# Turning the second tile's tokens through DRAM instead of on TensorE

## The chip, the cores and the metric

The kernel runs on one core of a Trainium2 chip. The metric is the device time of one execution in microseconds. TensorE does the matmuls, VectorE, ScalarE and GpSimd the element work, and SP (SyncE) issues nearly all the DMAs, one after another in the order of its own queue.

## The reference

Chunked attention over 8 batches of 576 tokens and 8 heads, followed by a gated feed-forward block over the 4608 tokens that come out of it:

```python
scores = scale * np.matmul(q_c, k_c.transpose(0, 1, 2, 4, 3))   # chunks of 64 tokens
attn = np.exp(scores - np.max(scores, axis=-1, keepdims=True))
attn = attn / (np.sum(attn, axis=-1, keepdims=True) + 1e-09)
out = np.matmul(attn, v_c)
x = out.transpose(0, 2, 1, 3).reshape(4608, 512)
xn = x / np.sqrt(np.mean(x * x, axis=-1, keepdims=True) + 1e-06) * rms_g
g = xn @ w_gate                                                  # 512 x 1536
silu = g * (1.0 / (1.0 + np.exp(-g)))
return (silu * (xn @ w_val)) @ w_out                             # 1536 x 512
```

## The kernel before

The tokens are worked off in nine tiles of 512. A tile consists of two units of 256 tokens, and a unit of two blocks of 128. Tiles 0, 1 and 2 are plain: for each of the 12 blocks `f` of the hidden width, `gate_and_value` makes two sums of 12 matmuls each (`ps_g`, `ps_v`), `gated` turns them into the product `sg` and splits it into a high and a low half (`gh`, `gl`), and `down` adds 12 matmuls to the four output sums `acc`. `down` of block f - 1 follows the gate of block f. At the end of a tile `evacuate` copies the four sums out, by turns on VectorE and ScalarE, and SP stores them (`out_dram<-o`). The six later tiles go in pairs with fewer products per pair; they read weights that were saved to DRAM (`wsd`, `osd`) during tiles 0 to 2.

Every product of full precision is made of three matmuls on high and low halves. Tile 0 therefore also converts the weights: the `conv_...` steps load 18 raw tiles (`raw`, 1 MB each) and split them into `parts`, with four operations a tile on VectorE (lines 201, 209, 217, 243) and three on ScalarE. Copies of the weights go to DRAM as `wfd`, `wsd` and `osd`.

The tokens of a tile are made by attention while the tile before is multiplied. Units 2 and 3 make tile 1, during tile 0; units 4 and 5 make tile 2, during tile 1; unit 6 belongs to the first pair and is begun at the start of tile 2: its loads are written at step 0 of that tile, its scores after the gate of f = 0. A unit loads `qt`, `kt` and `vt` (`load_unit`, 512 KB each, into the pool `io` of four buffers), makes scores, a softmax and the values, and `norm_unit` or `turned_norm` scales the rows. The matmuls want the tokens turned, with the model width on the partitions. For units 2 and 3 `norm_unit` writes into the tile `x`, GpSimd multiplies by the root mean square (line 517), and `x_transpose` turns 128 x 128 blocks on TensorE into PSUM at the end of tile 0, half of them ahead of the `down` of f = 10 and half ahead of that of f = 11. `x_split` then makes the halves `xh` and `xl`. For units 4 and later `turn_x` transposes 32 x 32 blocks in place on VectorE (line 458), sends the tile to DRAM (`away_x`), and `turn_x_back` fetches it in four reads of 32 partitions each, which land turned in `x`; there `x_split` works from `x`.

In tile 0 a scheduler sets the order on all engines. From tile 1 on TensorE keeps the order in which the code is written; the scheduler still orders SP, and may put a load ahead of work that is written earlier.

## Time and profile before

| What | Value |
|---|---|
| Median of three runs | 899.58 us (897.92 to 899.82) |
| Profiled execution, its own time | 898.29 us |
| Its span, first to last instruction | 896.5 us |
| TensorE busy | 880.0 us, 98% of the span |
| VectorE, ScalarE, GpSimd busy | 607.6, 454.1 and 185.7 us |
| Share of TensorE in the chain that ended last | 94% |
| Mean granted clock of TensorE | 0.991 |

Of 40 equal slices TensorE is full in 38; the first is the start-up. VectorE is full only in slices of tile 0, up to about 112 us. Tile 1 runs from 138 to 242 us, tile 2 begins there.

### The profile page before, as it was taken

What the parts mean: (1) busy time and instruction counts of PE and PEld (TensorE: products, weight loads), DVE (VectorE), ACT (ScalarE), POOL (GpSimd) and SP (SyncE); (2) the same over time, 40 slices, a digit from 0 to 9 for tenths busy, and PEclk for the clock granted to TensorE, in tenths of its full rate; (3) what the DMA queues carried; (4) which work ended last, traced back from release to release, by engine and by line L of the source; (5) the groups of instructions that cost most, each with busy time, mean ns of one, the idle gap of its engine ahead of it and who ended that gap; (6) DMA issues with size and microseconds to landing.
All of it is one profiled execution on the core that took longest, in us unless ns stands there. A gap on an engine that the chain in (4) does not pass through costs nothing.

```text
span 896.5 us, 17443 instructions
## 1 busy us (share of the span) xinstructions
PE 880.0 (98%) x6828; PEld 720.6 (80%) x6828; DVE 607.6 (68%) x965; ACT 454.1 (51%) x772; POOL 185.7 (21%) x157
## 2 busy tenths in 40 slices
PE   5999999999999999999999999999999999999998
PEld 4778888888888888888887888888878888888886
DVE  6999955364568745985677997556769953334776
ACT  5988934253446464454456645435547522222452
POOL 0004050342200000233233003333330014323200
PEclk8899999999999999999999999999999999999999
DMA  9889999777978855698977877677667794445442
GB/s 349 328 318 336 332 337 347 239 255 235 303 252 234 267 170 196 250 298 294 320 240 265 318 301 286 245 277 249 232 231 286 281 355 171 152 154 199 179 165 95
DMA packets 85794, 231.84 MB, mean 259 GB/s; under 512 B 8912, under 2 KB 45264, under 8 KB 71504
## 3 DMA queue, kind: packets, MB, share of 16 engines
q1 hardware_dynamic: 84656, 230.20, 73.1%
q8 instruction: 54, 0.88, 0.4%
q10 hardware_dynamic: 1056, 0.52, 0.2%
q14 instruction: 28, 0.23, 0.1%
HBM read 167.25 MB, written 63.44 MB: 257 GB/s over the span
## 4 chain that ended last, share of the span: by engine, by line
PE 94%; DVE 2%; ACT 2%; DMA 0%; issue 0%; POOL 0%; ACTq 0%; DVEq 0%
PE ps_b L857 11%; PE ps_a L857 11%; PE ps_c L857 11%; PE acc L664 11%; PE ps_g L627 11%; PE ps_v L627 10%; PE ps_b L1070 6%; PE ps_c L1070 6%; PE ps_d L857 5%; PE ps_a L1070 5%; PE ps_d L1070 3%; PE ps_o L426 2%; PE ps_s L299 2%; PE ps_o L484 1%; DMA x<-qT_dram 0%; ACT raw L196 0%
## 5 line engine op out<-in xcount | busy, mean ns | idle before, releaser
L857 PE MATMUL ps_b<-xp,wr 128*128 128x512 f32 x432 | 104.7, 391 | 0.1
L857 PE MATMUL ps_c<-xp,wr 128*128 128x512 f32 x432 | 104.0, 390 | 0.0
L857 PE MATMUL ps_a<-xp,wr 128*128 128x512 f32 x432 | 103.8, 390 | 0.0
L627 PE MATMUL ps_g<-xh,parts 128*128 128x512 f32 x288 | 97.2, 399 | 0.1
L857 PEld LDWEIGHTS ps_b<-xp,wr 128*128 128x128 f32 x432 | 80.5, 188 | 17.4 <-issue 0.5
L857 PEld LDWEIGHTS ps_c<-xp,wr 128*128 128x128 f32 x432 | 80.9, 188 | 16.9
L627 PE MATMUL ps_v<-xh,parts 128*128 128x512 f32 x288 | 94.5, 389 | 0.0
L857 PEld LDWEIGHTS ps_a<-xp,wr 128*128 128x128 f32 x432 | 80.8, 188 | 17.0
L664 PE MATMUL acc<-parts,gh 128*128 128x512 f32 x288 | 90.2, 394 | 0.0
L945 POOL TENSOR_TENSOR g<-u,u 128x512 f32<-128x512 f32 x18 | 23.2, 1289 | 251.9 <-DVE u L941 141.3
L627 PEld LDWEIGHTS ps_g<-xh,parts 128*128 128x128 f32 x288 | 54.7, 190 | 12.7 <-ACT parts L237 0.6
L627 PEld LDWEIGHTS ps_v<-xh,parts 128*128 128x128 f32 x288 | 54.1, 188 | 11.2
L977 ACT CAST gh<-g 128x512 fp32r<-128x512 f32 x72 | 43.6, 622 | 37.8 <-PE ps_c L1070 13.5
L664 PEld LDWEIGHTS acc<-parts,gh 128*128 128x128 f32 x288 | 53.1, 188 | 11.3
L982 DVE TENSOR_TENSOR gl<-g,gh 128x512 fp32r<-128x512 f32 x72 | 49.3, 692 | 16.2 <-PE ps_a L1070 5.7
L913 ACT ACTIVATE p<-p 128x512 f32<-128x512 f32 x36 | 22.7, 632 | 70.0 <-POOL p L935 60.4
L935 POOL TENSOR_TENSOR p<-p,p 128x512 f32<-128x512 f32 x36 | 46.9, 1313 | 53.9 <-DVE rs L387 35.6
L627 PE MATMUL ps_g<-xl,parts 128*128 128x512 f32 x144 | 56.8, 395 | 0.1
L664 PE MATMUL acc<-parts,gl 128*128 128x512 f32 x144 | 56.1, 390 | 0.0
L627 PE MATMUL ps_v<-xl,parts 128*128 128x512 f32 x144 | 56.0, 389 | 0.0
L922 DVE TENSOR_TENSOR u<-ps_b,p 128x512 f32<-128x512 f32 x36 | 24.6, 687 | 41.5 <-PE ps_b L857 38.0
L857 PE MATMUL ps_d<-xp,wr 128*128 128x512 f32 x216 | 52.3, 391 | 0.0
(151 smaller groups left out, 1706.7 us busy)
## 6 DMA issues: line engine op xcount, KB each, us to landing
wr<-wsd SPq DMA_DIRECT2D x63, 1024.0 KB, 7.0
wo<-osd SPq DMA_DIRECT2D x30, 1024.0 KB, 7.6
raw<-w_up_dram SPq DMA_DIRECT2D x12, 1024.0 KB, 9.5
vt<-v_dram SPq DMA_DIRECT2D x18, 512.0 KB, 7.2
wsd<-parts SPq DMA_DIRECT2D x18, 512.0 KB, 8.3
qt<-qT_dram SPq DMA_DIRECT2D x17, 512.0 KB, 5.6
kt<-kT_dram SPq DMA_DIRECT2D x17, 512.0 KB, 6.6
away_e<-e SPq DMA_DIRECT2D x28, 256.0 KB, 3.5
```

Of the source, the lines that this page charges most:

```text
L299: nc.tensor.matmul(st["s"][j][c * CH : (c + 1) * CH, pr], st["q"][rows, pr, tok : tok + CH], st["k"][rows, pr, tok : tok + CH], start=True ...
L426: nc.tensor.matmul(st["o"][(2 * c + t) * Q : (2 * c + t + 1) * Q, h * D : (h + 1) * D], eT[c][rows, t, h], vt[rows, c, h], start=True, sto ...
L627: nc.tensor.matmul(ps, a[f][:, cols], b[dt], start=(dt == 0 and i == 0), stop=(dt == NDT - 1 and i == 2),)
L664: nc.tensor.matmul(acc[s], a[:, cols], b, start=(f == 0 and i == 0), stop=(f == NF - 1 and i == 2),)
L857: nc.tensor.matmul(ps, w[:, a, m, cols], xp[:, b, kt], start=start and kt == 0 and i == 0, stop=stop and kt == 1 and i == 2, skip_group_ch ...
L913: nc.scalar.activation(t, t if src is None else src, AF.Silu)
L922: nc.vector.tensor_tensor(kp["u2"], b["b"], kp["p1"], op=add)
L935: nc.gpsimd.tensor_tensor(kp["p5"], kp["p1"], kp["p5"], op=add)
L945: nc.gpsimd.tensor_tensor(g[:, 0, 1], kp["u2"], kept[0]["u2"], op=mult)
L977: nc.scalar.copy(gh, src)
L982: nc.vector.tensor_tensor(gl, src, pair[0].bitcast(F32), op=ALU.subtract)
L1070: nc.tensor.matmul(banks[m][name], w[:, (0, 1, 0)[k], m * P : (m + 1) * P], (gh, gh, gl)[k], start=opens and i == 0 and k == 0, stop=not ( ...
```

## The change

Units 2 and 3 go the way of units 4 and later. `norm_unit` writes into a new tile `xu` of the pool `io`, which then holds four buffers for each unit; `turn_x` and `turn_x_back` of unit 2 are called at f = 7 and f = 8 of tile 0, those of unit 3 both at f = 10. `x_transpose` is gone. At f = 11 of tile 0 the gate's tail and the four splits are put in written order on ScalarE and VectorE. Unit 3's multiplication by the root mean square moves from GpSimd to ScalarE, unit 2's stays. The host undoes the changed order of tokens in the output from tile 1 on instead of tile 2.

```diff
-        first = 2 * u % NSUB
-        xu = x[:, first : first + 2]
-        xv = xu.rearrange("p s (j b a d) -> p j s b a d", j=2, b=2, d=Q)
+        xu = state["xu", u] = io.tile([P, 4, NDT, 2, Q], F32, tag="io", name="xu")
+        xv = xu.rearrange("p q (j b) s d -> p j s b q d", b=2)
+        xs = xu.rearrange("p q a s d -> p s (q a) d")
...
         for s in range(2):
-            nc.gpsimd.tensor_scalar(xu[:, s], xu[:, s], ri[:, s : s + 1], None, op0=ALU.mult)
+            if shared:
+                nc.scalar.mul(xs[:, s], xs[:, s], ri[:, s : s + 1])
+            else:
+                nc.gpsimd.tensor_scalar(xs[:, s], xs[:, s], ri[:, s : s + 1], None, op0=ALU.mult)
...
-    def x_transpose(dts):
-        for dt in dts:
-            pt = bank(ps_a, "ps_x")
-            for s in range(NSUB):
-                nc.tensor.transpose(
-                    pt[:, s * P : (s + 1) * P], x[:, s, dt * P : (dt + 1) * P], ident
-                )
-            x_split(dt, pt, slice(0, TT))
...
+    def next_tokens():
+        for dt in range(NDT):
+            x_split(dt, blocks(x)[:, :, dt], slice(0, TT))
...
+            elif t == 0 and f == NF - 1:
+                ps_last = gate_and_value(f)
+                with tc.manual_schedule(engines={mybir.EngineType.Activation, mybir.EngineType.DVE}):
+                    g = gated(f, CONVS[f % 2], conv_step, ps_last)
+                    next_tokens()
...
-                    norm_unit(u, o)
-                if f == NF - 1:
-                    x_transpose((0, 1))
+                    norm_unit(u, o, u == 3)
+                if f in (7, 10):
+                    turn_x(2 + (f == 10))
+                if f in (8, 10):
+                    turn_x_back(2 + (f == 10), x)
...
-        if t == 0:
-            x_transpose((2, 3))
```

**VectorE after the values of unit 3, in tile 0.** `ps_o` are unit 3's values, lines 209, 217 and 243 convert weights, the first `sg` and `gl` belong to f = 9. Before:

```order
L505 TENSOR_TENSOR x<-ps_o_1220,rs_u 128x2x128 x2
L209 SCALAR_TENSOR_TENSOR w<-w,raw 128x1024
L243 TENSOR_TENSOR parts<-w,parts 128x1024
L217 SCALAR_TENSOR_TENSOR w<-raw,w 128x1024
L209 SCALAR_TENSOR_TENSOR w<-w,raw 128x1024
L243 TENSOR_TENSOR parts<-w,parts 128x1024
L217 SCALAR_TENSOR_TENSOR w<-raw,w 128x1024
L651 TENSOR_TENSOR sg<-ps_v,sg 128x512
L243 TENSOR_TENSOR parts<-w,parts 128x1024
L656 TENSOR_TENSOR gl<-sg,gh 128x512
```

After:

```order
L505 TENSOR_TENSOR xu<-ps_o_1224,rs_u 128x2x4x32 x2
L209 SCALAR_TENSOR_TENSOR w<-w,raw 128x1024
L243 TENSOR_TENSOR parts<-w,parts 128x1024
L217 SCALAR_TENSOR_TENSOR w<-raw,w 128x1024
L201 TENSOR_SCALAR w<-w 128x1024
L458 STREAM_TRANSPOSE xu<-xu 128x1024
L209 SCALAR_TENSOR_TENSOR w<-w,raw 128x1024
L645 TENSOR_TENSOR sg<-ps_v,sg 128x512
L217 SCALAR_TENSOR_TENSOR w<-raw,w 128x1024
L650 TENSOR_TENSOR gl<-sg,gh 128x512
L243 TENSOR_TENSOR parts<-w,parts 128x1024 x2
```

One conversion tile's work has moved behind the `sg` of f = 9, and a clamp (line 201) and the block transpose of `xu` stand ahead of it.

**SP in tile 0, around a pair of raw weight loads.** `wsd` are stores of converted weights, `wfd` copies of the weights, `qt` and `kt` the loads of unit 3. Before:

```order
L222 DMA wfd_133<-w 128x1024
L182 DMA raw<-w_up_dram 128x1024 x2
L687 DMA wsd_141<-parts 128x4x256
L687 DMA wsd_143<-parts 128x4x256
L222 DMA wfd_134<-w 128x1024
```

After:

```order
L222 DMA wfd_133<-w 128x1024
L182 DMA raw<-w_up_dram 128x1024 x2
L267 DMA qt<-qT_dram 128x1024
L268 DMA kt<-kT_dram 128x1024
L222 DMA wfd_134<-w 128x1024
```

The loads of unit 3 stand where two stores were; before they stood far ahead of these rows, and the two stores are now earlier.

**SP at the end of tile 1.** `away_x` and the reads back are unit 5's tokens, the first `qt` is the load of unit 6, the one behind `out_dram` that of unit 7. Before, a stretch around the loads and one around the stores:

```order
L754 DMA w<-wfd_139 128x1024
L267 DMA qt<-qT_dram 128x1024
L461 DMA away_x_2423<-xu 128x1024
L268 DMA kt<-kT_dram 128x1024
L269 DMA vt<-v_dram 128x1024
L468 DMA x<-away_x_2423 32x4x256 x4
L778 DMA wsd_160<-side 128x512
```

```order
L780 DMA wsd_159<-w 128x2x256
L967 DMA out_dram<-o 128x512 x4
L267 DMA qt<-qT_dram 128x1024
L849 DMA wr<-wsd_140 128x2048
L268 DMA kt<-kT_dram 128x1024
```

After, the same two stretches:

```order
L748 DMA w<-wfd_139 128x1024
L461 DMA away_x_2422<-xu 128x1024
L681 DMA wsd_157<-parts 128x4x256
L681 DMA wsd_159<-parts 128x4x256
L681 DMA wsd_160<-parts 128x4x256
L736 DMA osd_162<-parts 128x2x256
L736 DMA osd_165<-parts 128x2x256
L736 DMA osd_171<-parts 128x2x256
L468 DMA x<-away_x_2422 32x4x256 x4
L772 DMA wsd_160<-side 128x512
```

```order
L774 DMA wsd_159<-w 128x2x256
L961 DMA out_dram<-o 128x512 x4
L267 DMA qt<-qT_dram 128x1024
L268 DMA kt<-kT_dram 128x1024
L269 DMA vt<-v_dram 128x1024
L267 DMA qt<-qT_dram 128x1024
L843 DMA wr<-wsd_140 128x2048
```

The three loads of unit 6 have moved from ahead of the reads to behind the four output stores, where the first `qt` is now unit 6's and the second unit 7's; six stores of weights stand between unit 5's way out and its reads.

## Rows read from the trace of the kernel before

**Rows 1.** The page's busy times: engine, us, share of the span, instructions.

```profile
PE 880.0 (98%) x6828; PEld 720.6 (80%) x6828; DVE 607.6 (68%) x965; ACT 454.1 (51%) x772; POOL 185.7 (21%) x157
```

**Rows 2.** Waits of TensorE: us in total, times, longest; first and last of five.

```profile
PE ps_s L299 <- DMA x<-qT_dram: 5.6, 2, 5.1
...
PE ps_a L1070 <- DVE gl L982: 0.3, 1, 0.3
```

**Rows 3.** Timeline of TensorE, end of tile 0: start us, us, line, operation.

```profile
131.02 1.03 PE L533 MATMUL ps_x<-ident,x 128*128 128x128 f32 x8
...
138.24 0.39 PE L627 MATMUL ps_g<-xh,parts 128*128 128x512 f32 x1
```

**Rows 4.** The chain that ended last, in order of time: one undisturbed `down` block.

```profile
123.02 2.72 PE acc L664 x12
```

**Rows 5.** Instructions on tile `xu` up to 220 us: ns min/median/max.

```profile
L452 ACT ACTIVATE xu<-xu,ri x2: 712/718/724, 183.1 to 184.2; 128x512 f32<-128x512 f32 x2
L458 DVE STREAM_TRANSPOSE xu<-xu x1: 1246/1246/1246, 184.9 to 184.9; 128x1024 f32<-128x1024 f32 x1
```

**Rows 6.** Timeline, 114 to 121 us.

```profile
114.55 5.63 POOL L517 TENSOR_SCALAR x<-x,ri_u 128x512 f32<-128x512 f32 x2
...
118.75 0.68 DVE L651 TENSOR_TENSOR sg<-ps_v,sg 128x512 f32<-128x512 f32 x1
...
120.14 0.39 PE L627 MATMUL ps_v<-xh,parts 128*128 128x512 f32 x1
```

**Rows 7.** DMA issues by line, whole run: count, KB each, median us to landing.

```profile
away_x<-xu SPq DMA_DIRECT2D x14, 512.0 KB, 3.0
x<-away_x SPq DMA_DIRECT2D x56, 128.0 KB, 4.3
```

**Rows 8.** Timeline, 66 to 80 us.

```profile
67.55 1.18 SPq L687 DMA_DIRECT2D wsd<-parts  x2
...
78.59 1.16 PE L299 MATMUL ps_s<-kt,qt 64*64 64x64 f32 x64
```

**Rows 9.** DMA issues near 33.6, 68, 233 and 245 us: us to landing.

```profile
qt<-qT_dram SPq DMA_DIRECT2D x1, 512.0 KB, 10.0
...
wsd<-parts SPq DMA_DIRECT2D x2, 512.0 KB, 11.5
...
x<-away_x SPq DMA_DIRECT2D x1, 128.0 KB, 5.6
...
qt<-qT_dram SPq DMA_DIRECT2D x1, 512.0 KB, 3.7
```

**Rows 10.** Timeline of SP's issues, 224 to 246 us.

```profile
224.78 0.45 SPq L267 DMA_DIRECT2D qt<-qT_dram  x1
...
231.70 1.75 SPq L468 DMA_DIRECT2D x<-away_x  x4
...
245.33 0.44 SPq L267 DMA_DIRECT2D qt<-qT_dram  x1
```

**Rows 11.** Timeline, 239 to 249 us.

```profile
239.75 2.56 ACT L524 ACTIVATE xh<-x,g_col 128x512 fp32r<-128x512 f32 x4
...
242.31 0.39 PE L627 MATMUL ps_g<-xl,parts 128*128 128x512 f32 x1
...
247.62 1.16 PE L299 MATMUL ps_s<-kt,qt 64*64 64x64 f32 x64
```

**Rows 12.** Busy times, 220 to 240 us; last: clock, DMA share, GB/s.

```profile
220.00:240.00 20.00, 20.00 (x113) 16.52 (x98) 8.89 (x14) 8.70 (x19) 6.63 (x6) 1.00 1.02 315
```

**Rows 13.** Tile `kt`: us from issue to landing over all its loads.

```profile
DMA to landing us min/median/max: 3.5/6.6/9.4
```

**Rows 14.** Three start-up stretches; the clock is third from the end.

```profile
16.00:18.00 2.00, 0.66 (x4) 0.42 (x4) 1.86 (x6) 1.36 (x3) 0.12 (x1) 0.87 0.99 418
28.00:30.00 2.00, 1.91 (x5) 1.42 (x5) 2.00 (x6) 2.00 (x5) 0.00 (x0) 0.50 0.96 389
30.00:32.00 2.00, 2.00 (x8) 1.53 (x7) 1.93 (x3) 1.96 (x3) 0.00 (x0) 0.72 0.81 330
```

## Prediction

> **What bounds the kernel now.** I read the busy times first. TensorE is busy for 880.0 us, 98% of the span [rows 1]. Next comes the list of what TensorE waited for: its five entries add up to 12.3 us and all but the last lie in the start-up, before the long matmuls of tile 0 begin [rows 2]. After that it waits 0.3 us in all. So the time is the sum of what stands in TensorE's own queue, and only two things can move it: instructions taken out of that queue, or a new wait put into it. A saving on VectorE, ScalarE or GpSimd is worth nothing here, and a wait of TensorE is paid in full, since no slack follows that could take it back.

> **The change, part by part.** *Sixteen transposes leave TensorE.* In the timeline they begin at 131.02, the two last `down` blocks stand among them, and tile 1 begins at 138.24 [rows 3]: 7.22 us. One undisturbed `down` block of 12 matmuls takes 2.72 us in the chain [rows 4], two take 5.44. The rest, 1.78 us, is what the transposes cost, and nothing hides it. This is the gain, and its only source: -1.8 us.

> *What replaces them lies beside TensorE.* VectorE gets two block transposes of 1.25 us, ScalarE two multiplications of 0.72 us for unit 3 [rows 5], GpSimd loses two of its own. VectorE has little room in tile 0. The tightest place is the product `sg` of f = 9: it ends at 118.75 + 0.68 = 119.43, and TensorE reuses that bank at 120.14 [rows 6], 0.7 us later. The order on VectorE shows six weight-conversion operations between the normalisation of unit 3 and that product before, and now four of them, a clamp and the block transpose, which is no more work. I take nothing for it; if the cover were gone, a block transpose of 1.25 us less 0.7 leaves 0.5 us.

> *Unit 3's way through DRAM.* GpSimd began the scale at 114.55 [rows 6]; on ScalarE it can end near 116, and the transpose near 117.3. With the medians of 3.0 us for the way out and 4.3 us for the way back [rows 7] and four issues of some 0.4 us, the tokens are back near 127. Tile 1 begins at 138.24 - 1.78 = 136.5, and the split ahead of its first low-half matmul takes some 1.5 us, so they are needed at 135. With a cover of 8 us I put it at nothing.

> *The queue of SP, first place: unit 3's q and k.* Their loads stood far ahead in the queue; now they follow two raw weight loads, where two stores of converted weights were issued from 67.55 on, so k goes out at about 68.2. The scores that read them run at 78.59 [rows 8], now behind two `down` matmuls, so near 79.05. A q load in the same position behind two raw loads took 10.0 us, the two stores a median of 11.5 [rows 9]: landing at 78.2 or 79.7, a wait of nothing or 0.7 us. I take the row of the load, which is the same transfer: 0, with 0.7 kept as the upper end.

> *Second place: the tokens of unit 5, which open tile 2.* Before, k and v of unit 6 (1.05 MB) stood between the way out and the four reads back, and the last read, issued near 233.1, landed 5.6 us later [rows 9, 10], at 238.7. Tile 2's first low-half matmul is at 242.31 and needs one split on ScalarE, where four take 2.56 us, and one on VectorE, some 1.5 us together [rows 11], so reads landing by 240.8 are in time: slack 2.1 us. In the changed order six stores of 2.36 MB stand there instead, 1.31 MB more. The DMA engines are full from 220 to 240 us and move 315 GB/s [rows 12], so the reads come 4.2 us later against everything else, and tile 2 starts 2.1 us late. Ends: nothing, if the reads overtake the stores, and 4.2 us, if the slack is used up elsewhere. I take +2.1.

> *Third place: q and k of unit 6.* This is the dearest line. Before, q of unit 6 went out at 224.78 [rows 10], 23 us ahead of its scores at 247.62 [rows 11]. In the changed order all three loads of unit 6 stand behind the four output stores of tile 1, and the last of these waits for the last evacuation of the tile. SP issues in order, so the load cannot go earlier. The load of unit 7's q stood in just that place before: issued at 245.33, landed after 3.7 us [rows 9, 10]. Everything moves 1.78 us forward with TensorE: q of unit 6 goes out at 243.55 and lands at 247.25; k, 0.52 MB behind it at 315 GB/s, 1.66 us later, at 248.9. The scores are due at 247.62 - 1.78 = 245.84, and TensorE's order is fixed from tile 1 on, so it stands still for 3.1 us. Ends: k issued at 244.0 with the shortest, the median and the longest landing of any k load, 3.5, 6.6 and 9.4 us [rows 13], gives 1.7, 4.8 and 7.6 us. If tile 2 starts late, the evacuations stand behind the same splits on ScalarE and the stores move too, so the two waits add up. [...]

> *Sum:* -1.8 + 0 + 2.1 + 3.1 = +3.4 us. The profiled execution took 898.29 us, so it would take 901.7; the median of the runs before is 899.58, so I put the median after at 903.0.

> **The rivals.** *Only unit 6 is late.* The reads of unit 5 overtake the stores in the DMA engines, or the stores move faster than 315 GB/s, and tile 2 starts on time. For it: no row shows stores and reads of this mix end in the order of issue. Against it: before, reads at the same place took 5.6 us against a median of 4.3 [rows 7, 9], so they do stand behind what was issued ahead of them. Then -1.8 + 3.1 = +1.3, or 900.9; with the shortest k landing -0.1, or 899.5.

> *The loads are covered, and the kernel is faster.* One mechanism: unit 6's k lands before TensorE asks for it, and only the removal of the transposes is left, 897.8 us. It decides at a landing within 1.8 us of the issue at 244.0, or if SP reached the loads 2 us sooner than the evacuations let it. No k load in the trace landed in under 3.5 us [rows 13], and the stores have to come first; so little speaks for it.

> [...]

> **How the numbers follow.** The forecast, both waits: 0.49. Only unit 6 late: 0.24. Covered: 0.12. Clock falls: 0.15. A difference of 0.2%, 1.8 us, is about what a measurement of this kernel can tell from no change. Slower by more than that: the forecast except its low end (0.43), the clock (0.15), the upper end of unit 6 alone (0.03), together 0.61. Faster by more: the covered case lies at -1.8, just on the edge, 0.08 of its 0.12. Within 0.2%: 0.31. The range reaches from 899.2, a little under unit 6 alone with the shortest landing, to 906.0, the forecast with the median k landing (4.8 instead of 3.1) and 1.3 us more from the other upper ends; it leaves out the covered case and the far ends of the landings.

> **What the profile after would show.** The sixteen `ps_x` matmuls of tile 0 gone, and its last `down` block running straight into tile 1. In the list of TensorE's waits a new entry: scores (`ps_s`) waiting for a DMA, `kt` or `qt`, once, near 246 us and 2 to 5 us long; if it is missing, the main step is wrong. A second, smaller one at the first `ps_g` of tile 2, near 240 us, put down to the splits `xh` or `xl`, which in turn wait for the reads `x<-away_x`; if the splits do not wait, only the third place is real. A wait of `ps_s` near 79 us would show the first place to have no cover. [...] The prediction is wrong if TensorE's wait in tiles 1 and 2 stays under 1 us in all, or if a wait appears in tile 0 from VectorE's queue.

## The result, and the profile after

The changed kernel takes 912.23 us (median of 6 runs, 907.59 to 914.81) against 899.19 us (6 runs, 897.56 to 900.31): 1.0138 times as long, 95% interval 1.0109 to 1.0167. The forecast was 903.0 us with a range up to 906.0. It had the sign; the loss is 13 us instead of 3.4.

Here is the page's busy row, which answers to [rows 1], and the list of what TensorE waited for, which answers to [rows 2] (us in total, times, longest; entries of the start-up left out):

```profile
PE 883.6 (97%) x6812; PEld 721.2 (79%) x6812; DVE 615.7 (68%) x967; ACT 456.0 (50%) x774; POOL 175.7 (19%) x155
```

```profile
PE ps_s L299 <- DMA kt<-kT_dram: 3.9, 1, 3.9
...
PE ps_o L426 <- DMA eT<-away_e: 1.0, 3, 0.5
PE ps_o L426 <- issue: 0.8, 1, 0.8
...
PE ps_g L621 <- DVE xl L528: 0.6, 2, 0.3
PE ps_g L621 <- DVE parts L243: 0.3, 1, 0.3
```

The 16 matmuls are gone (x6828 before), and there are waits where there were none. But the waits listed are 6.6 us, the span is 10.7 us longer (907.2 against 896.5), and TensorE is busy 3.6 us longer with less to do. Part of the added busy time is slower work: 64 score matmuls that took 1.16 us, at a granted clock of 1.00 from 246 to 250 us, took 1.99 at 0.50 from 254 to 256 us. So I read the traces as a ladder: the start of the same instruction in both timelines, and the difference. Where the difference steps, time was lost or won. All times in us; the first column is the time in the kernel before, "again" is a second trace of the changed kernel (below).

| instruction | before | changed | again |
|---|---|---|---|
| unit 2's second scores | 41.22 | +1.41 | +0.75 |
| unit 3's values | 105.31 | +1.98 | +1.08 |
| unit 4's scores (tile 1) | 149.22 | +0.19 | -0.71 |
| unit 5's values | 218.78 | +0.19 | -0.71 |
| unit 6's scores (tile 2) | 247.62 | +6.35 | +6.47 |
| unit 7's scores | 265.25 | +8.87 | +8.02 |
| unit 11's values (first pair) | 413.33 | +9.53 | +8.02 |
| unit 12's scores | 420.86 | +11.44 | +14.42 |
| unit 17's values | 658.89 | +10.82 | +13.82 |
| end of the span | 896.5 | +10.7 | +17.3 |

Five steps. The start-up (+1.4) is not the change's: all programs are alike there, and the granted clock was still 0.50 from 32 to 34 us and 0.95 from 34 to 36, where the kernel before had 0.72 from 30 to 32 and 1.00 from then on; the other traces below that have nothing new there give 0.0 to 1.6. Another 0.6 comes at 83 us, where a matmul waits for converted weights. Between 105 and 149 the transposes go: 1.98 to 0.19, that is -1.79. The two that cost are the start of tile 2, about +8.7, and **a place in the first pair that the prediction does not name at all**, +1.9 in one trace and +6.4 in the other.

**The first place.** TensorE's timeline of the changed kernel, at tile 2's start (start us, us, line, operation, idle time before it and its releaser):

```profile
243.97 0.50 PE L621 MATMUL ps_g<-xl,parts 128*128 128x512 f32 x1 [0.29 <-DVE xl L528]
...
245.22 0.50 PE L621 MATMUL ps_g<-xl,parts 128*128 128x512 f32 x1 [0.29 <-DVE xl L528]
...
253.97 1.99 PE L299 MATMUL ps_s<-kt,qt 64*64 64x64 f32 x64 [3.91 <-DMA kt<-kT_dram]
255.89 0.79 PE L621 MATMUL ps_g<-xh,parts 128*128 128x512 f32 x1
```

The same 64 score matmuls took 1.16 us before [rows 11]. The issues of SyncE (SP in the rows), which answer to [rows 10]: stores, reads of unit 5, output stores, and only then unit 6's keys.

```profile
230.16 2.73 SPq L681 DMA_DIRECT2D wsd<-parts  x3
232.93 3.88 SPq L736 DMA_DIRECT2D osd<-parts  x3
236.91 2.48 SPq L468 DMA_DIRECT2D x<-away_x  x4
...
244.94 3.54 SPq L961 DMA_DIRECT2D out_dram<-o  x4
248.57 0.38 SPq L267 DMA_DIRECT2D qt<-qT_dram  x1
249.00 0.43 SPq L268 DMA_DIRECT2D kt<-kT_dram  x1
```

And the clock there (from and to, us, TensorE busy, granted clock, DMA share, GB/s), which answers to [rows 14] and to the chance of 0.15 that the clock falls:

```profile
246.00:250.00 4.00, 4.00 (x18) 1.00 1.00 344
250.00:254.00 4.00, 0.09 (x5) 0.83 0.93 348
254.00:256.00 2.00, 2.00 (x65) 0.50 1.06 438
256.00:258.00 2.00, 2.00 (x5) 0.50 1.03 424
258.00:260.00 2.00, 2.00 (x7) 0.63 0.97 365
260.00:264.00 4.00, 4.00 (x19) 1.00 0.19 77
```

After the wait TensorE works at a granted clock of 0.50 until about 259.5 (an estimate from the mean of 0.63 from 258 to 260 us, if 0.50 gives way to 1.00 in one step). That adds 2.52 us to the wait (6.35 to 8.87 in the ladder).

**The second place.** In the second trace TensorE stops inside the value products of unit 11, one matmul short of the end, and the trace knows no releaser ("issue"). It does so again in unit 17's:

```profile
421.35 1.48 PE L426 MATMUL ps_o<-vt,eT 64*32 64x64 f32 x127
427.54 0.26 PE L426 MATMUL ps_o<-vt,eT 64*32 64x64 f32 x1 [4.72 <-issue]
427.73 4.65 PE L851 MATMUL ps_a<-xp,wr 128*128 128x512 f32 x11
```

```profile
672.71 1.40 PE L426 MATMUL ps_o<-vt,eT 64*32 64x64 f32 x119
676.45 0.32 PE L426 MATMUL ps_o<-vt,eT 64*32 64x64 f32 x9 [2.34 <-issue]
```

Two theories for the first place, each with a number to lose. **Q**: it is the order in SyncE's queue. **W**: it is the added work itself. For the second place, **F**: TensorE's own program arrives late. The page of the changed kernel lists a queue that moves instructions (packets, MB, share):

```profile
q8 instruction: 54, 0.88, 0.4%
```

0.88 MB in 54 packets is 16 KB a packet. If they carry the 13,624 matmuls and weight loads of TensorE in equal shares, and 53 would not be enough, a packet holds 253 to 257 of them; 256 is an estimate within these bounds. The value products of a unit are 128 matmuls and 128 weight loads, by this estimate just one packet's worth, done in 1.5 us. Take 16 transposes and their 16 weight loads out of the program, and every later cut between packets falls 32 instructions further on in the work. **D**, its rival: the turned probabilities are read back late.

### The profile page after: what moved, and what is told of

Its sections match the earlier page's. It is cut to its first block, busy times and chain, and to the rows that moved or that the text cites. A ratio compares the mean times of both kernels' runs of the same rounds, so it can differ in the third digit from the quotient of the medians.

```text
span 907.2 us, 17434 instructions
## 1 busy us (share of the span) xinstructions
PE 883.6 (97%) x6812; PEld 721.2 (79%) x6812; DVE 615.7 (68%) x967; ACT 456.0 (50%) x774; POOL 175.7 (19%) x155
## 4 chain that ended last, share of the span: by engine, by line
PE 88%; DVE 5%; DMA 3%; ACT 2%; issue 1%; POOL 1%; SPq 0%; ACTq 0%; DVEq 0%
PE ps_g L621 11%; PE ps_a L851 10%; PE ps_b L851 10%; PE ps_c L851 10%; PE ps_v L621 10%; PE acc L658 9%; PE ps_b L1064 5%; PE ps_c L1064 5%; PE ps_a L1064 5%; PE ps_d L851 5%; PE ps_d L1064 3%; PE ps_o L426 2%; PE ps_s L299 2%; DMA wr<-wsd 1%; DVE w L209 1%
```

## The experiments

Each ran beside the kernel before on the same chip; the medians of the kernel before were 898.4 to 899.0 us there. The plain stores are the 36 stores of converted weights (`wsd` and `osd` from `parts`) that `save_plain` writes out, six at a call.

### SyncE's queue: four runs

*All plain stores early in tile 1:*

```diff
-                if f % 2 == 0:
-                    save_plain(f // 2)
+                if f < NPR:
+                    save_plain(f)
```

> The changed kernel with the 36 stores of plain weight parts written out at one index per step (f = 0 to 5) instead of every second step. The issue queue of SyncE then has all of them ahead of unit 5's way through DRAM, and unit 6's queries and keys ahead of unit 5's reads and of tile 1's output stores. Theory Q (the loss is SyncE's queue order at the end of tile 1): the 3.9 us wait of unit 6's first scores and the waits of the first gate in tile 2 go, the granted clock stays at 1.00 there, and about 8.7 us come back: span 897 to 899, time 898 to 902 us. Theory W (the loss is the added work itself: 1.25 us turns on VectorE, eight more DMAs in tile 0, ScalarE's two scalings): the same work remains, so the time stays at 909 to 914.

Measured 910.08 us, 1.0120 (1.0099 to 1.0142). At unit 6's scores the ladder stands at +5.35, from -0.91 at unit 5's values: the wait for kt is gone and another has come, 2.9 us of `acc` for ScalarE's `gh`. SyncE issued the last loads of converted weights at 227.3 instead of 224.3, so GpSimd's sums began at 234.49 (229.27 before), ScalarE's copies of them came late, and `gh` stands behind these copies in ScalarE's order. The clock at 245 to 250 us is 0.74. Then +6.2 at the second place. The time is outside Q's range and inside W's, but 6.2 us of it lie at the second place, for which neither had a term: the ladder decides, not the time. In it Q had the wait right and not what stood next.

*Unit 6's loads ahead of the stores:*

```diff
+            at[19].append(lambda: load_unit(6))
...
-                    at.setdefault(max(UNIT_AT[n] + after_it[k], 0), []).append(f)
+                    if n or k:
+                        at.setdefault(max(UNIT_AT[n] + after_it[k], 0), []).append(f)
```

> The changed kernel with unit 6's three loads written out one step ahead of unit 5's reads, so that they stand ahead of the six stores, of these reads and of the output stores in SyncE's queue; nothing else moves. Theory Q: the 3.9 us wait for kt goes, and with it the 2.5 us at the low clock that followed; the first gate of tile 2 stays late by 1 to 3 us, or by 3 to 5 if 1.5 MB of loads go ahead of the reads: 903 to 908 us. If the clock fell for another reason than that wait, only 3.9 us come back and matmuls near 256 us still take twice as long. Theory W: 909 to 914.

Measured 913.75 us, 1.0178 (1.0141 to 1.0215). The wait for kt is gone; in its place the first gate of tile 2 waits 5.0 us for `xh`, since unit 5's reads stand behind 1.5 MB of loads and six stores and take 5.5 to 7.2 us to land (3.3 to 3.7 in the changed kernel). The clock fell all the same, to 0.50 from 248 to 252. So the low clock does not belong to that one wait. The time is again outside Q's range: Q had one wait right and the price of the other too low, and 6.4 us lie at the second place.

*Unit 5's reads ahead of most of the stores:*

```diff
+            at[19].extend(at.pop(20))
             half = Steps(at)
```

> The changed kernel with unit 5's four reads written out in the same step as its store to DRAM, so that four of the six stores stand behind them; unit 6's loads stay behind the output stores. Theory Q: the first gate of tile 2 starts at once (at most 0.2 us of waits for xh or xl), so the output stores and unit 6's loads move with it, but the scores are then due earlier by as much: the wait for kt stays at 3 to 5 us, with the low clock behind it; 2 us come back at most: 908 to 912 us. Theory W: no change, 909 to 914.

Measured 912.54 us, 1.0151 (1.0125 to 1.0176). As Q expected, there is no wait for `xh` or `xl`; but the wait for kt is 8.1 us in two pieces, the longest 6.7, instead of 3 to 5, and the ladder is at +9.33 after unit 6, from -0.24. The time is 0.5 us above Q's range, with 7.2 us at the second place.

*The kernel before, with unit 6's loads behind tile 1's output stores and nothing else changed:*

```diff
+                    if n or k:
+                        at.setdefault(max(UNIT_AT[n] + after_it[k], 0), []).append(f)
...
+            if t == 1:
+                with tc.manual_schedule(engines={mybir.EngineType.SP}):
+                    evacuate(acc, t, s)
+                    if s == NSUB - 1:
+                        load_unit(6)
```

(The loads are taken out of tile 2's steps and put in a fixed order on SyncE with the four output stores.)

> The kernel before, with one part of the change's effect alone: unit 6's loads are written out behind tile 1's four output stores, in that order in SyncE's queue; transposes, stores and buffers as before. Theory Q: unit 6's first scores, due at 247.6, wait for keys issued near 246 to 247 us that land 5 us later: a wait of 3.5 to 5 us and then 2 to 3 us at the low clock: 904 to 907 us. The prediction's price for this place was 3.1 us with nothing for the clock: 902.3 us. Theory W: no loss, 898 to 900.

Measured 903.23 us, 1.0053 (1.0034 to 1.0072). TensorE's waits, and the clock behind them:

```profile
PE ps_s L299 <- DMA kt<-kT_dram: 3.5, 2, 3.1
```

```profile
246.00:250.00 4.00, 2.52 (x12) 1.00 0.99 316
250.00:252.00 2.00, 0.39 (x25) 1.00 1.00 397
252.00:254.00 2.00, 2.00 (x58) 0.59 1.05 436
254.00:256.00 2.00, 2.00 (x7) 0.55 0.98 389
```

The waits are 3.5 us, the ladder steps by 4.75 (+0.83 to +5.58), and 1.6 of it lie behind the scores, at the low clock. This one part of the change, alone in the old kernel, costs what the forecast said and the clock on top; the time is 0.8 us below Q's 904 and clear of W's 898 to 900. There is no step at unit 11's values.

### TensorE's program: six runs

*Sixteen small transposes into TensorE's idle time at 23.6 us of the changed kernel, read by nobody (the pad, from here on):*

```diff
+        for b in two_banks(ps_acc, "ps_pad"):
+            for k in range(8):
+                nc.tensor.transpose(b[:Q, 0, :Q], ident[:Q, :Q], ident[:Q, :Q])
         for d in range(0, NDT, 2):
             x_turn_unit(1, d, ps_acc)
```

> The changed kernel with 16 transposes of a 32x32 corner of the identity put into TensorE's order at 23.6 us, where it idles 2 us for a scale of ScalarE: the sixteen instructions that the change took out of TensorE's program are in it again, nothing reads their result, and SyncE's queue is in the same order as in the changed kernel. Theory F (second place of loss: the program's 16 KB instruction blocks; without the 16 transposes a block ends with the 256 instructions of unit 11's value products, which last 1.5 us, so that TensorE waits there for the next block; 1.9 us in the changed kernel's trace at 423 to 426 us, 5.0 us in the run with the early stores): the step after unit 11's values loses nothing against the kernel before, no idle time without a releaser there, the 8.7 us at tile 2's start stay: 2 to 7 us come back, 905 to 910 us. Theory D (the loss there is late data, the turned probabilities read back from DRAM): it stays, 909 to 914.

Measured 907.21 us, 1.0104 (1.0089 to 1.0120), 5 us less than the changed kernel. The ladder passes unit 11's values at +10.61 and reaches the next scores at +10.70: no step, no idle time without a releaser. The step at tile 2's start stays, +8.8.

*The kernel before without the sixteen transposes (tile 1's tokens are left unturned):*

```diff
-            pt = bank(ps_a, "ps_x")
-            for s in range(NSUB):
-                nc.tensor.transpose(
-                    pt[:, s * P : (s + 1) * P], x[:, s, dt * P : (dt + 1) * P], ident
-                )
-            x_split(dt, pt, slice(0, TT))
+            x_split(dt, blocks(x)[:, :, dt], slice(0, TT))
```

> The kernel before without the 16 transposes of tile 1's tokens (the halves are made from the unturned tokens: this turning is left out); units 2 and 3, ScalarE, VectorE and all transfers but two output stores' places as before. Without theory F only the transposes' 1.8 us go: 897 to 898 us. With theory F the kernel loses 2 to 7 us after unit 11's values near 411 us although nothing but TensorE's program has changed: 899 to 905 us, and the idle time there has no releaser in the trace or a read of turned probabilities as its last.

Measured 906.75 us, 1.0086 (1.0052 to 1.0121): **taking work out of TensorE, and nothing else of the change, makes the kernel 8 us slower.** (In SyncE's order three plain stores have also moved behind tile 0's output stores; they stand there in the next run too, which does not lose.) The ladder is flat at -0.18 from tile 1 to unit 11's values, then +6.66. The timeline there, and the one of the kernel before, whose products run through:

```profile
413.15 1.47 PE L426 MATMUL ps_o<-vt,eT 64*32 64x64 f32 x127
419.29 0.31 PE L426 MATMUL ps_o<-vt,eT 64*32 64x64 f32 x1 [4.67 <-issue]
419.53 5.33 PE L852 MATMUL ps_a<-xp,wr 128*128 128x512 f32 x12
```

```profile
413.33 1.92 PE L426 MATMUL ps_o<-vt,eT 64*32 64x64 f32 x128
415.18 3.02 PE L857 MATMUL ps_a<-xp,wr 128*128 128x512 f32 x12
```

The instruction queue's packets in this stretch (queue, packets, MB, share): without the transposes one falls between 416 and 417, while TensorE stands; in the kernel before it falls between 410 and 411, before the products begin.

```profile
q8 instruction: 1, 0.02, 6.2%
```

```profile
q8 instruction: 1, 0.02, 7.4%
```

An estimate from the counts says what the sixteen change. Without them one packet of the program covers unit 11's products almost exactly: it begins at their start and ends behind the 127th. With them every packet begins 32 instructions earlier in the work, so this one ends behind the 111th product and begins some 17 matmuls ahead of the first, 3.9 us at 0.23 us each. If the next packet is asked for when one begins, it has these 3.9 us more to arrive; when it is asked for, no run shows.

And behind the stop the lower clock again: 12 matmuls in 5.33 us instead of 3.02, 0.50 granted from 419 to 423.

*The same with sixteen, 128 and 144 small transposes at 23.6 us (the diff of the pad, with 8, 64 and 72 in a bank):*

> The kernel before without the 16 transposes of tile 1's tokens (as in the run without them: this turning is left out), and 16 small transposes put at 23.6 us. Theory F: the 6.8 us at unit 11's values go, only the removed transposes' 0.8 to 1.8 us are left: 897 to 898.5 us. If the loss came from reordered stores or the like, which are as in the run without the pad: 903 to 907.

Measured 898.83 us, 1.0006 (0.9995 to 1.0017). No step at unit 11 (+0.91 to +0.45).

> The kernel before without the 16 transposes of tile 1's tokens (that turning is left out), with 128 small transposes at 23.6 us instead of 16: 256 instructions, one whole block of TensorE's program. Theory F: the blocks end where they do without any, so the stall after unit 11's values is there, 5 to 7 us from its begin to the full clock, with no releaser. Rival (any additional instructions or a shift in time help): no stall. The start is up to 2 us later, since 128 of them take longer than the 2 us of idle time; some stores of tile 0 change places.

> The same with 144 small transposes: one whole block and the sixteen. Theory F: no stall after unit 11's values (under 0.5 us), so 5 to 7 us less than with 128, although there are more instructions. Rival: as with 128.

Measured 913.06 us with 128 (1.0165, 1.0143 to 1.0187) and 904.96 us with 144 (1.0063, 1.0046 to 1.0080): sixteen transposes more, 8 us less. So many of them cost time where they stand: by tile 1 the ladders are at +4.6 and +7.9. At unit 11 the one steps by 5.9, the other by 0.7, and at unit 17 by 4.5 and 0. Timelines of the two, at unit 11:

```profile
417.90 1.47 PE L426 MATMUL ps_o<-vt,eT 64*32 64x64 f32 x126
423.80 0.27 PE L426 MATMUL ps_o<-vt,eT 64*32 64x64 f32 x2 [4.43 <-issue]
```

```profile
422.46 1.42 PE L426 MATMUL ps_o<-vt,eT 64*32 64x64 f32 x122 [0.26 <-DMA eT<-away_e]
423.81 3.02 PE L852 MATMUL ps_a<-xp,wr 128*128 128x512 f32 x12
```

With 256 added instructions the stop returns to its place, two matmuls from the end of the burst; with 288 it is gone. Both move 55 packets on the instruction queue where all other traces have 54. A mere shift in time would not come back with the count of 256; a program cut every 256 instructions does. F holds, and the traces tie stop and packet together. In the nine traces that step at unit 11, TensorE goes on 2.2 to 2.8 us after a packet of the instruction queue starts, whether that packet comes early or late: 423.7 and 426.48 in the first trace of the changed kernel, 417.0 and 419.29 in the kernel before without transposes, 425.3 and 427.54 in the second trace of the changed kernel. The six stops at unit 17 do the same. In the traces that do not step, the last packet before unit 11's products starts 3.1 to 6.6 us ahead of them.

Why the packet comes 0.8 to 4.7 us behind the start of the burst was not tried. The transfers are full in that stretch (in the run without transposes 1.00 of the DMA engines and 413 GB/s from 415 to 419), and where it came after 0.8 us they were not (0.35 and 96 GB/s from 422 to 424 in the first trace of the changed kernel); that would fit a packet that waits among other transfers, which no run shows by itself.

*The changed kernel itself once more:*

> The changed kernel itself, for a second trace. If the stall after unit 11's values is a fetch that takes its turn among the other transfers, it varies from run to run: between 1.9 us (first trace) and 7 us (the runs with the same order there), while the 8.7 us at tile 2's start stay within 1 us.

Measured 914.48 us (2 runs); the trace is the one shown above. 6.4 us at unit 11, 3.5 more at unit 17, 8.7 at tile 2's start. The stop varies from run to run. The first trace had met a short one: 0.8 us with no releaser, and 1.0 us in three pieces put down to the probabilities' way back, as theory D had it, with the clock at 1.00 throughout. Whether these 1.0 us are the change's stays open. The short stop fits the times: the traced run took 908.94 us, the median is 912.23.

### Both mended, and where the stores can go

*Plain stores moved past tile 1 (the 18 of indices 3 to 5 written out at steps 3 to 5 of tile 2; in the trace nine of them come behind tile 1, the rest before):*

> The changed kernel with the last 18 of the 36 stores of plain weight parts (indices 3 to 5) written out in tile 2 instead of tile 1; the transfers read weights that tile 2 still uses and are needed from the first pair on. SyncE's queue has unit 5's way through DRAM and unit 6's queries and keys ahead of tile 1's output stores, and nothing of the plain parts between them. Theory Q (SyncE's queue at the end of tile 1 and the load on the DMAs there make the first loss): offset at unit 6's scores falls from +6.2 to within 1 us of that at tile 1's start, and no low clock behind it: about 8 us come back, less whatever the second place takes (2 to 7 us): 900 to 905 us. Theory W (the added work itself): 909 to 914.

Measured 906.93 us, 1.0106 (1.0082 to 1.0130). Unit 6's scores stand at +0.37, from -0.56, so the first loss is gone as Q has it; the rest is +2.3 at unit 10 and +5.5 at unit 11, and the time lies between Q's range and W's.

*Both edits:*

> Both edits together: 18 stores in tile 2, and 16 small transposes in TensorE's idle time at 23.6 us. Theories Q and F together: neither loss is left, and the 1.8 us of the removed transposes show: 896 to 899 us, same or slightly faster than the kernel before (899.2). If only one of them holds: 901 to 906.

Measured 901.26 us, 1.0029 (1.0016 to 1.0043), 11 us under the changed kernel: neither large step is left in the ladder, so Q and F together account for them. But the time is above the 896 to 899 of both theories. What is left is the start-up (+1.2), 0.8 us at tile 2's start and 2.0 us at unit 10's values, which now wait for the probabilities' way back (`eT<-away_e`, 1.4 us).

*Units 2 and 3 keep their rows in x, 30 of the 36 stores are written out at the end of tile 0 and six at the first step of tile 1, pad:*

```diff
-        xu = state["xu", u] = io.tile([P, 4, NDT, 2, Q], F32, tag="io", name="xu")
+        place = x[:, 2 * u % NSUB : 2 * u % NSUB + 2].rearrange("p s c -> p (s c)")
+        xu = state["xu", u] = place.rearrange("p (q a s d) -> p q a s d", q=4, a=NDT, s=2)
...
+            if t == 0 and f == NF - 2:
+                for i in range(NPR - 1):
+                    save_plain(i)
+            if t == 1 and f == 0:
+                save_plain(NPR - 1)
             if t == 1:
-                if f % 2 == 0:
-                    save_plain(f // 2)
...
```

> The changed kernel with three edits that give back the order of before: units 2 and 3 write their rows into their own half of x instead of a buffer of the load pool (so unit 3's loads are early again), all 36 stores of plain weight parts are written out at the end of tile 0 (so SyncE's queue from tile 1's end on stands as in the kernel before), and 16 small transposes stand in TensorE's idle time at 23.6 us (so its instruction blocks end where they did). Theories Q and F: no loss at tile 2's start nor after unit 11's values, and 1.8 us of transposes gone: 896.5 to 899 us against 898.5 to 899.2 of the kernel before. If 2 MB of additional transfers in tile 0 and tile 1 cost something by themselves (theory W in part), 900 to 905.

Measured 912.78 us, 1.0166 (1.0152 to 1.0180): a miss. From tile 2 on the ladder is flat, as built. But the stores now stand ahead of unit 4's loads, whose keys are issued at 154.11; TensorE waits 8.0 us for them and works at the low clock behind (0.50 from 161 to 164 us), +13 at tile 1's start. The loss has only moved.

*The same without the pad:*

> The same without the 16 small transposes. Theory F: the loss after unit 11's values is back, 4 to 7 us near 412 to 418 us with no releaser in the trace, and nothing else: 901 to 906 us. Without theory F: as with them, 896.5 to 899.

Measured 920.10 us, 7.3 us more. In the trace, of a run of 924.09 us, unit 11 steps by 7.3 (+16.09 to +23.36) and unit 17 by some 3.

*Rows of units 2 and 3 in a buffer of the load pool again, pad:*

> As the mended kernel, pad included, but units 2 and 3 keep their rows in a buffer of the load pool as the changed kernel does, so unit 3's queries and keys stand behind two loads of raw weights. The prediction's price for that place: 0 (upper end 0.7). In the ladder of the changed kernel against before the scores of unit 3 and what follows them are 0.5 us later: 0.5 us more than the mended kernel, all of it between 62 and 100 us.

Measured 912.49 us, the same as with rows in x. Its ladder gains 0.45 at unit 3's scores and the other one the same 0.45 a little later, so the 0.5 us expected did not come: the place in the queue of unit 3's loads is worth nothing that these runs can tell.

*Half of the stores late in tile 2:*

> As the mended kernel (rows of units 2 and 3 in x, 16 small transposes at 23.6 us), but the plain stores of indices 0 to 2 as in the changed kernel and those of 3 to 5 written out at steps 6, 8 and 10 of tile 2; 12 stores are then left in tile 1 and 9 come after it. If only order and room on the transfers count: no loss of over 1 us at tile 1's or tile 2's start, none after unit 11's values, 897 to 900 us. If stores anywhere displace something as dear: 901 to 906.

Measured 902.05 us, 1.0032 (1.0016 to 1.0048): +0.4 at tile 2's start, none of the large steps; small ones of 0.2 to 1.8 us in tile 2 and the first pair. That is the second of the two forecasts.

*All stores early in tile 1:*

> As the mended kernel, but all 36 stores written out in the first three steps of tile 1, behind unit 4's loads and the first loads of the converted weights; 21 stores stand in tile 1, and unit 4's loads ahead of them. If only the order counts: tile 1's start and unit 6's scores lose under 1 us, 897 to 900 us. If tile 1 lacks the transfer time for 21 stores: the chain from the loads of converted weights over GpSimd's sums to ScalarE's copies is 2 to 3 us late near 237 us as in the run with the early stores, and 4 to 6 us are lost there: 902 to 906.

Measured 907.62 us, 1.0094 (1.0077 to 1.0111): with 21 stores early in tile 1 it is unit 5's scores that come late (3.3 us of waiting for kt; +5.5, then +2.9 more), a place that neither forecast named.

So the stores are the load that has to go somewhere. Both programs write them out in tile 1, and the scheduler that orders SP moves some ahead: in the kernel before, 30 of the 36 stand ahead of tile 0's output stores and six right behind; in the changed kernel it is 15 and 21. Why the scheduler chose so is not shown. What the traces show of tile 0 is that SyncE's queue now waits at a store for VectorE's turn and at the reads for that store, and everything behind waits with it. These are its new waits from 84 to 125 us (those for converted weights, 16.4 us, were 16.0 before):

```profile
SPq L468 <- DMA away_x<-xu: 3.7, 2, 2.5
...
SPq L461 <- DVE xu L458: 1.7, 1, 1.7
```

In tile 0 the transfers are less full: DMA share and GB/s in three stretches, of the changed kernel and of the one before.

```profile
105.00:110.00 5.00, 1.00 0.69 195
110.00:115.00 5.00, 1.00 0.66 201
115.00:120.00 5.00, 1.00 0.44 179
```

```profile
105.00:110.00 5.00, 1.00 0.93 337
110.00:115.00 5.00, 1.00 1.05 342
115.00:120.00 5.00, 1.00 0.92 320
```

15 us at some 140 GB/s less are about 2 MB that did not move in tile 0, and tile 1 is fuller: 297 GB/s from 140 to 240 us against 270. How much of that comes from the waits and how much from the stores' new places was not tried apart. No version tried beats the kernel before. The run without transposes but with the pad suggests why none would by much: with the turning free and left out, and the program's cuts where they were, it is at 1.0006.

## Why the prediction was wrong, point by point

**Step 1, the transposes, -1.8: this is the step that failed.** Their own time was right, -1.79 in the ladder (in the two runs that only leave them out 0.8 and 0.7, where a `down` then waits 0.5 us for `gl`). What the step left out is that instructions which leave a program move all those behind them. It counted the sixteen matmuls by their time on TensorE only. The run that makes this one edit alone costs +8 us, and the two that put sixteen or 144 others in show it to be the cut of the program. In the changed kernel this is 1.9 to 6.4 us at unit 11 (of the 1.9, 1.0 may be late data) and up to 3.5 at unit 17, no part of the sum nor of a rival.

**Step 2, VectorE and ScalarE, 0 (at most 0.5):** right in the main. One new wait of 0.31 us in tile 0, for converted weights from VectorE, costs 0.6 in the ladder. The prediction had called a wait from VectorE's queue there a sign that it is wrong; but the wait is also in the kernel before without transposes and with the pad (0.2 us), and not in the second trace of the changed kernel, so it is not the change's own. Theory W, this work as the cause, fell with the run that moves nine stores and adds the pad and has all of the work.

**Step 3, unit 3's way through DRAM, 0:** right as to TensorE. Turn at 117.44, reads issued from 121.65 to 123.40, tile 1 starts at 138.44 without a wait. If it cost something, that stands on SyncE, in the queue behind its store: the step looked at who waits for the tokens, and not at what is queued behind the waiting store.

**Step 4, unit 3's keys, 0 (at most 0.7):** right. Issued at 69.51, landed after 10.0 us as the row of [rows 9] said, scores at 80.45.

**Step 5, unit 5's tokens, +2.1:** near in size and not in mechanism. The first gate starts 0.9 us late (243.18 against 242.08 and 0.19) and takes 4.00 us instead of 2.72: 2.2. But the bytes ahead of the reads did not hold them up once they were issued. From issue to landing the four reads took less than in the kernel before; first the changed kernel, then the one before:

```profile
DMA to landing us min/median/max: 3.3/3.5/3.7
DMA to landing us min/median/max: 5.6/5.8/5.8
```

They were late at their issue, the last at 239.0 instead of 233.0. Unit 5's way out was issued at 229.79 instead of 227.81, behind a turn on VectorE that began 2.0 us late, and issuing the six stores then held SyncE from 230.16 to 236.81. That these terms come to nearly the forecast of 2.1 is luck.

**Step 6, unit 6's keys, +3.1:** right in mechanism, 0.8 short: 3.9. The wait stands where the prediction put it in the list, and is one of 2 to 5 us. The keys went out at 249.00, since the output stores ended only at 248.48; the landing took 4.8 us. From the issue of q at 248.57 to the landing of k it was 5.2 us.

**The sum left out the clock.** Its fall had a chance of 0.15, as a case by itself. An estimate from [rows 14] gives +1.6 us for it: at 0.50 from 28 us on, and back at 1.00 near 31.1 if the mean of 0.72 from 30 to 32 us is one step, TensorE loses half of 3.1 us. It is no other case, it comes on top: +2.5 us in the changed kernel, 1.6 in the run with only unit 6 late. That no such wait lies outside the start-up before was no reason to give it 0.15: the start-up's rows were the only ones there were, and they showed a clock of 0.50. Behind the waits of 3.9 and 3.1 us here it was 0.50 (254 to 258 us) and 0.55 to 0.59 (252 to 256 us).

With these, the steps and the clock come to -1.8 + 0.6 + 2.2 + 3.9 + 2.5 = +7.4 us, as against 7.5 between the ladder's +1.41 and +8.87; the second place makes the rest.

## What to carry to other kernels

When a kernel is bound by one engine's instruction stream, look where its bursts of short instructions lie: here a burst of 128 matmuls and 128 weight loads in 1.5 us, by estimate as long as one packet of the program, ran out of instructions for 0.8 to 5.0 us, and 32 instructions put in far ahead of it ended that; adding or taking a few idle instructions is a cheap experiment, and it told this cause from late data and from a shift in time. When a new transfer waits in an in-order queue, follow what is queued behind it to where it comes out, since these transfers then stand in front of others that had been early. And price a wait of TensorE with the slow stretch behind it, here 2.5 us behind 3.9 and 1.6 behind 3.5.
